# Row blocks coupled across tile and batch ends, and a new order of seats and gathered rows between dense and expert products

## The chip, the cores and the metric

The kernel runs on one core of one Trainium2 chip. The metric is the device time of one execution in microseconds (us). TensorE is PE in the rows (PEld: its weight loads), VectorE DVE, ScalarE ACT, GpSimd POOL, and SyncE, which issues most DMAs, SP.

## The reference

Four batches of attention with 12 heads, 448 rows, head size 64, whose scores are mixed over the heads before the softmax and whose weights are mixed after it; then a dense layer pair with ELU on 1792 tokens; then eight experts, each token to one or to none.

```python
scores = scale * np.matmul(q, k.transpose(0, 1, 3, 2))
scores = np.einsum('bhij,hg->bgij', scores, w_pre)
attn = np.exp(scores - np.max(scores, axis=-1, keepdims=True))
attn = attn / (np.sum(attn, axis=-1, keepdims=True) + 1e-09)
x = np.matmul(np.einsum('bhij,hg->bgij', attn, w_post), v)   # rows of 768
h = x @ w_in
x = np.where(h > 0.0, h, np.exp(np.minimum(h, 0.0)) - 1.0) @ w_out
# where x @ w_skip > 0: e = argmax(x @ w_gate), p = its softmax weight
out = x + p * (np.maximum(x @ w1[e], 0.0) @ w2[e])           # else x
```

## The kernel before

**Attention.** A tile is 120 query rows of a batch, or its last 88 (`ROWS`): 16 tiles `T`. `qk` (L153) makes the scores of two heads ("a pair", six a tile) and moves them, one head on ScalarE, one on VectorE, into `st[T]`; two such buffers alternate. Mixing over heads is done on row blocks of up to 10 rows (`blocks_of`, L76): `relayout` (L187) brings a block with its 12 heads onto the partitions by DMA, `mix_pre` (L201) multiplies two blocks, a *couple* `U`, with the spread-out mixing matrix, `top`, `softmax` and `norm` do the rest, and `mix_post` (L251) mixes again, transposed, into two PSUM tiles `f`, whose blocks `move` copies to `att[T]`. `av` (L275) multiplies two heads' weights with the values. The 88-row tile was cut into eight blocks of 10 and two of 4.

A *unit* `n` of the loop (L399) is up to two couples of one tile, three units a tile, so the last unit of each batch has one couple. TensorE's order in a unit, by hand: `mix_pre` of its couples, `mix_post` of the former unit's first couple, one `av`, two `qk`, `mix_post` of the former unit's second couple. `when` gives by division which tile's pairs, keys and queries are due. `split_k` and `high_q`/`low_q` split keys and queries in two parts. `qk` and `mix_pre` share four PSUM buffers `w` in turn. In the last five units (`late`) the score pools are closed (`scoring.close`) and the dense layer is begun in steps (`next(mix)`): weights are loaded (L530), narrowed (L541 to L553), x is loaded and split. Each engine works in order; up to `order.close()` (in the dense layer) the order is that of the program, behind it a scheduler's, which `behind` (an instruction goes out after a named one) holds.

**Between dense and expert products.** The second dense product goes by tiles of 128 tokens (L918). For each tile `route` picks the expert, `seat` (L829) counts how many earlier tokens go there (`ones` x `seen`), adds those of its tile (`upper` x one-hot), and scatters the token to its slot. Expert 0's first 128 rows are not read back from memory alone: `xp` holds rows gathered for the first 12 tiles, and the rows of tile 12 (`OLD`) and tile 13 (`LAST`) are added by products with a 0/1 place matrix `hot` (`place_old`, L884, and L963) in PSUM `pt`, 12 instructions each. The last tile's logits go over transposed copies (`score_turned`, `logits`).

## Time and profile before

| | us |
|---|---|
| timed runs | 994.80, 988.57, 992.12 |
| median | 992.12 |
| profiled execution | 988.09 |
| its span, first to last instruction | 986.2 |
| TensorE / VectorE / ScalarE / GpSimd busy | 963.5 / 722.0 / 550.9 / 233.5 |
| mean granted clock of TensorE | 0.996 of full speed |

The profile is one execution. A busy share is an average over stages with different limits, and the end of a matmul is modelled, so a busy TensorE is not one at its peak. In a timeline a row tells the start, the length, the engine, the line and operation, what it writes and reads, how many were merged, and in brackets how long its engine stood idle before it and who ended that. Units of the loop are told apart by the first `mix_pre` of each (L206).

### The profile page before, as it was taken

Reading aid. Unit: us, or ns where it says so; the run is one execution under the profiler, and the core shown is the slowest. Engines: PE = TensorE matmul, PEld = TensorE weight load, DVE = VectorE, ACT = ScalarE, POOL = GpSimd, SP = SyncE. Lnnn points to the kernel's source line nnn. Section 1 sums busy time; section 2 is a strip of 40 time slices with the busy share of each in tenths; the row PEclk is TensorE's granted clock in tenths of the full one; section 3 lists DMA queues with packets and bytes.
Section 4 is the critical chain, followed back from the end, with each engine's and each line's share of the span. In section 5 each row is a group of like instructions: output and inputs, shape, how many; then the busy total and the mean of one; then the engine's idle time right before and its main releaser. Section 6 shows DMA issues by size and latency. Waiting matters only on the chain. (4 is left out here: it accounts for less than half of the span.)

```text
span 986.2 us, 30114 instructions
## 1 busy us (share of the span) xinstructions
PE 963.5 (98%) x12286; PEld 838.7 (85%) x12286; DVE 722.0 (73%) x1458; ACT 550.9 (56%) x1113; POOL 233.5 (24%) x291
## 2 busy tenths in 40 slices
PE   9999999999998999999999999999999999999996
PEld 4677777777776789998999999999999998898985
DVE  6777777777776786666666478877686847999973
ACT  4887788788786754444554453222212106788861
POOL 2333234234222322223233100010100004252001
PEclk9999999999999999999999999999999999999999
DMA  6674674574557565445666389643333387999910
GB/s 202 219 237 145 216 234 156 198 240 153 195 190 234 175 207 184 157 161 169 219 225 211 137 292 290 175 126 97 118 97 100 104 294 264 394 394 397 391 71 34
DMA packets 129160, 199.86 MB, mean 203 GB/s; under 512 B 31924, under 2 KB 95863, under 8 KB 128764
## 3 DMA queue, kind: packets, MB, share of 16 engines
q1 hardware_dynamic: 126812, 191.60, 58.1%
q0 software_dynamic: 2160, 6.31, 1.7%
q8 instruction: 97, 1.59, 0.7%
q14 instruction: 43, 0.35, 0.1%
q10 hardware_dynamic: 48, 0.00, 0.0%
HBM read 122.66 MB, written 37.35 MB: 162 GB/s over the span
## 5 line engine op out<-in xcount | busy, mean ns | idle before, releaser
L918 PE MATMUL o<-w,gh 128*128 128x384 f32 (+2 forms) x1344 | 238.2, 336 | 0.0
L636 PE MATMUL h<-xh,w 128*128 128x448 f32 x1152 | 235.4, 366 | 1.6 <-DVE xh L572 1.3
L918 PEld LDWEIGHTS o<-w,gh 128*128 128x128 f32 x1344 | 232.0, 188 | 2.2
L636 PEld LDWEIGHTS h<-xh,w 128*128 128x128 f32 x1152 | 215.7, 188 | 20.2 <-DVE xh L572 1.9
L214 DVE TENSOR_REDUCE nmx<-c 128x1 f32<-128x448 f32 x184 | 102.3, 617 | 51.9 <-PE c L206 51.8
L266 PEld LDWEIGHTS f<-kr,e 64*64 64x64 f32 x5888 | 105.3, 135 | 36.6 <-issue 22.3
L227 ACT ACTIVATE e<-c,nmx 128x448 f32<-128x448 f32 x184 | 114.5, 633 | 25.5 <-DVE nmx L214 25.4
L805 DVE SCALAR_TENSOR_TENSOR junk<-x,wrow 128x768 f32<-128x768 f32 x117 | 111.8, 955 | 18.4 <-ACT x L948 12.8
L247 POOL TENSOR_SCALAR kr<-kpost,rs 128x60 f32<-128x60 f32 x184 | 79.4, 455 | 183.9 <-DVE rs L242 90.6
L1086 DVE TENSOR_TENSOR wlo<-w1t,whi 128x1536 fp32r<-128x1536 f32 x64 | 110.8, 1751 | 10.7 <-ACT whi L1084 8.9
L266 PE MATMUL f<-kr,e 64*64 64x60 f32 (+1 forms) x5888 | 108.3, 219 | 2.9 <-issue 1.8
L553 POOL TENSOR_TENSOR wf<-a,p 128x768 f32<-128x768 f32 x32 | 66.1, 2066 | 181.1 <-DVE p L551 139.4
L1084 ACT CAST whi<-w1t 128x1536 fp32r<-128x1536 f32 x64 | 93.8, 1483 | 21.5 <-PE y L1126 9.4
L790 ACT CAST gh<-gr 128x512 fp32r<-128x512 f32 x56 | 34.8, 624 | 97.1 <-PE o L918 35.5
L206 PE MATMUL c<-d,kpre_low 64*64 64x448 f32 x368 | 84.1, 547 | 0.3 <-DMA d<-s 0.2
L206 PE MATMUL c<-d,kpre_up 60*64 60x448 f32 x368 | 81.6, 548 | 0.0
L272 ACT COPY at<-f 128x420 f32<-128x420 f32 (+1 forms) x136 | 65.6, 518 | 28.0 <-PE f L266 27.2
L294 PE MATMUL xp<-at,v 128*64 128x120 f32 (+1 forms) x1152 | 67.1, 264 | 3.1 <-issue 3.0
L853 POOL DMA_INDIRECT slots<-pairs,si x14 | 18.9, 1348 | 204.6 <-DVE si L852 152.7
L166 PE MATMUL qk<-k,qq 64*120 64x448 f32 x504 | 65.3, 381 | 0.7 <-ACT e L227 0.2
L294 PEld LDWEIGHTS xp<-at,v 128*64 128x64 f32 x1152 | 56.1, 137 | 10.6 <-issue 9.3
L170 ACT ACTIVATE s<-qk 120x448 f32<-120x448 f32 x96 | 52.2, 548 | 23.1 <-PE qk L166 14.6
(204 smaller groups left out, 1278.7 us busy)
## 6 DMA issues: line engine op xcount, KB each, us to landing
w1t<-in_moe_w_dram SPq DMA_DIRECT2D x64, 768.0 KB
d<-s SPq DMA_DIRECT2D x176, 210.0 KB
gT<-g SPq DMA_DIRECT2D x64, 224.0 KB
f<-in_moe_w_in_dram SPq DMA_DIRECT2D x16, 768.0 KB
f<-in_moe_w_out_dram SPq DMA_DIRECT2D x16, 768.0 KB
gr<-gT SPq DMA_DIRECT2D x48, 256.0 KB
rq<-in_q_dram SPq DMA_DIRECT2D x15, 360.0 KB
rk<-in_k_dram SPq DMA_DIRECT2D x24, 224.0 KB
```

Source lines behind the costliest of these rows:

```text
L206: nc.tensor.matmul(out=ps[j * UP:(j + 1) * UP, :S], lhsT=kpre_up[UP:UP + HP, :] if z else kpre_low, rhs=d[z, j])
L214: nc.vector.tensor_reduce(out=t, in_=c, op=ALU.max, axis=AX.X, negate=True)
L227: nc.scalar.activation(out=e, in_=c, func=ACTF.Exp, bias=t, accum_out=sms[0][:, k + i:k + i + 1])
L247: nc.gpsimd.tensor_scalar(out=kr, in0=kposts[z], scalar1=rs[:, 2 * i + z:2 * i + z + 1], scalar2=None, op0=ALU.mult)
L266: nc.tensor.matmul(out=ps[to, heads, z, :], lhsT=e[rows, keys * JW:(keys + 1) * JW], rhs=kr[rows, first * HR:(first + n) * HR])
L294: nc.tensor.matmul(out=ps[i][z * 64:(z + 1) * 64, :n], lhsT=vt[b, p][:, jc * 2 + z, :], rhs=att[T][:, jc * H + ORDER.index(2 * p + z), :n] ...
L553: nc.gpsimd.tensor_tensor(out=w, in0=a, in1=p, op=ALU.add)
L636: nc.tensor.matmul(out=ps, lhsT=w[:, a, kk, :], rhs=xs[tb, kk][:, z, :], start=(kk == 0 and a + z == 0), stop=(kk == NK - 1 and a == 1))
L805: nc.vector.scalar_tensor_tensor(out=t[:, o:o + n], in0=x2, scalar=1.0, in1=w, op0=ALU.mult, op1=ALU.mult, accum_out=lg[:, e:e + 1])
L918: mm = nc.tensor.matmul(out=po[c][:, :cols[c].stop - cols[c].start], lhsT=gs[i][fc // GC][:, a, fc % GC, :], rhs=wo[fc][:, z, cols[c]], st ...
L1084: nc.scalar.copy(out=hi, in_=t)
L1086: nc.vector.tensor_tensor(out=lo, in0=t, in1=hi, op=ALU.subtract)
```

## The change

Blocks of a tile are 10 rows and one rest (12, 12, 12, 9 a batch). Couples and units are cut from the whole list of blocks, whatever tile or batch a block is of: 180 blocks, 90 couples, 45 units of two couples. `begins` and `ends` tell the first and last couple of a tile; from them two lists are made: `pairs_in` (which score pairs a unit computes: two, in six units three, none in the last five) and `values_in` (which `av`: one, twice two, three in the last unit). Loads and splits of keys and queries follow `pairs_in`. A `mix_post` writes its two blocks where each belongs. In unit 40 both relayouts of unit 42 are issued before the score pools close, so unit 41 issues none of them. The `av` in the last unit after the first two uses two of the buffers `w`.

Behind the dense products `place_old` is cut in two: `place_pre` (the gathered rows `xp`, no place matrix needed) and `place_old` (tile 12's rows). `seat` is cut too: `counted` makes the product with `seen`, and in `seat` the place matrix comes ahead of the sums' rest; the weight's reciprocal (`weigh`) is put behind it for tiles 12 and 13. All products of the stage are put in one order by `behind`: two of `place_pre`, transposes, the seat product of tile 12, two of `place_pre`, logits, the last two of `place_pre`, two of `place_old`, the seat products of tile 13, four of `place_old`, then the products of tile 13's rows.

```diff
-    whole = n // BR * BR
-    few = (n - whole) // 2
-    return [(r, BR) for r in range(0, whole, BR)] + [(whole + i * few, few) for i in range(2 if few else 0)]
+    return [(r, min(BR, n - r)) for r in range(0, n, BR)]
...
         blks = [(T, r, m) for T in range(len(tiles)) for r, m in blocks_of(ROWS[tiles[T][1]][1])]
-        units = []
-        for T in range(len(tiles)):
-            Gs = [G for G in range(len(blks)) if blks[G][0] == T]
-            Us = list(zip(Gs[::2], Gs[1::2]))
-            units += [Us[2 * u:2 * u + 2] for u in range(3)]
+        Us = list(zip(range(0, len(blks), 2), range(1, len(blks), 2)))
+        units = [Us[i:i + 2] for i in range(0, len(Us), 2)]
         NP = len(units)
+        begins = [[T for T, _, _ in blks].index(T) // 2 for T in range(len(tiles))]
+        ends = [U - 1 for U in begins[1:]] + [len(Us) - 1]
+        for T in range(1, len(tiles)):
+            if blks[2 * begins[T]][0] != T:
+                ends[T - 1] = begins[T]
...
+
+        pairs_in, values_in = {}, {}
+        for T in range(1, len(tiles)):
+            n1 = begins[T] // 2 - (2 if begins[T] % 2 else 3)
+            n0 = n1 - 2
+            if T > 1:
+                gone = ends[T - 2]
+                n0 = max(n0, gone // 2 - (1 if gone % 2 else 2), max(pairs_in) + 1)
+            if T == len(tiles) - 1:
+                n1 -= 1
+            ns = range(n0, n1 + 1)
+            for p in range(NK):
+                pairs_in.setdefault(ns[p * len(ns) // NK], []).append((T, p))
+        for T in range(len(tiles) - 1):
+            n0 = max(ends[T] // 2 + 2, max(values_in, default=0) + 1)
+            n1 = min(begins[T + 2] // 2 + 1 if T + 2 < len(tiles) else NP - 1, n0 + 2)
+            for u in range(3):
+                values_in.setdefault(min(n0 + u, n1), []).append((T, u))
...
                 T, r, m = blks[G]
-                whole = ROWS[tiles[T][1]][1] // BR * BR
-                t = r // BR if r < whole else (whole // BR) + (r - whole) // m
-                rows = st[T][:PR].rearrange("(a t) h s -> t a h s", a=BR)[t][:m]
+                rows = st[T][:PR].rearrange("(a t) h s -> t a h s", a=BR)[r // BR][:m]
...
-            T, r, m = blks[U[0]]
-            if r == 0:
-                att[T] = at_p.tile([128, NA, 120], FP32, tag="at", name="at")
+            for G in U:
+                if blks[G][1] == 0:
+                    att[blks[G][0]] = at_p.tile([128, NA, 120], FP32, tag="at", name="at")
...
             def move(copy, j):
+                T, r, m = blks[U[j]]
...
                 first = HR - m // 2
-                copy(out=to[:, :, r + j * m:r + (j + 1) * m], in_=at[:, :, first:first + m])
+                copy(out=to[:, :, r:r + m], in_=at[:, :, first:first + m])
...
-        def when(n):
-
-            return n // 3, n % 3
-
+        def first_in(n):
+
+            return [T for T, p in pairs_in.get(n, ()) if p == 0]
+
+        def fresh(n):
+
+            return [(tiles[T][0], p) for T, p in pairs_in.get(n, ()) if tiles[T][1] == 0]
...
             new = units[n + 1] if n + 1 < NP else ()
-            T, u = when(n + 5)
-            T1, u1 = when(n + 6)
-            T2, u2 = when(n + 7)
-            for U in new[1:]:
-                relayout(U)
+            now = pairs_in.get(n, [])
+            new_q = [(T, p // 2) for T, p in now if T >= PLAIN and (T, p // 2) not in qt]
+            new_q = [x for i, x in enumerate(new_q) if x not in new_q[:i]]
+            if n != NP - 4:
+                for U in new[1:]:
+                    relayout(U)
             store()
-            if n == NP - 5:
-                scoring.close()
...
             del values[:2 if n else 0]
-            if T2 < len(tiles):
-                if u2 == 0:
-                    load_q(T2)
-                if tiles[T2][1] == 0:
-                    load_k(tiles[T2][0], 2 * u2)
-                    load_k(tiles[T2][0], 2 * u2 + 1)
-            if PLAIN <= T < len(tiles):
-                high_q(T, u)
+            for T in first_in(n + 2):
+                if T > 1:
+                    load_q(T)
+            for b, p in fresh(n + 2):
+                load_k(b, p)
+            for x in new_q:
+                high_q(*x)
...
                     relayout(units[n + 2][0])
+            if n == NP - 5:
+                relayout(units[n + 2][1])
+                scoring.close()
...
                 top(U)
-            if PLAIN <= T < len(tiles):
-                low_q(T, u)
+            for x in new_q:
+                low_q(*x)
...
             moves, scores = [mix_post(U) for U in old[:1]], []
-            weighted = [av((n - 1) // 3 - 1, (n - 1) % 3)] if n >= 4 else []
-            if T < len(tiles):
-                scores.append(qk(T, 2 * u))
+            weighted = [av(*x) for x in values_in.get(n, ())[:1]]
+            if now:
+                scores.append(qk(*now[0]))
...
                 next(mix)
-            keys = (tiles[T1][0], 2 * u1, nc.gpsimd) if T1 < len(tiles) and tiles[T1][1] == 0 else ()
+            keys = [(*bp, nc.gpsimd) for bp in fresh(n + 1)]
             if n < 3:
-                keys = 0, 2 * n, nc.vector
-            if keys:
-                split_k(*keys)
+                keys = [(0, 2 * n + i, nc.vector) for i in range(2)]
+            for x in keys[:1]:
+                split_k(*x)
...
                 f()
-            if T < len(tiles):
-                scores.append(qk(T, 2 * u + 1))
+            for f in scores[:len(now) - 2]:
+                f()
+            scores = scores[max(len(now) - 2, 0):]
+            for x in now[1:]:
+                scores.append(qk(*x))
...
                 f()
-            if keys:
-                split_k(keys[0], keys[1] + 1, keys[2])
+            for x in keys[1:]:
+                split_k(*x)
...
                 m[0](nc.scalar.copy)
-            if n == NP - 1:
-                av(n // 3 - 1, n % 3)()
+            for i, x in enumerate(values_in.get(n, ())[1:]):
+                av(*x, *([[ps_w.tile([128, 512], FP32, tag="w", name="xp") for _ in range(2)]] if i else []))()
...
                 nc.scalar.activation(out=ex, in_=lg[:, :E], func=ACTF.Exp, bias=nmx, accum_out=sm)
-                nc.vector.tensor_scalar(out=sm, in0=sm, scalar1=1e-9, scalar2=None, op0=ALU.add)
-                nc.vector.reciprocal(out=pairs[:, i, 1:2].bitcast(FP32), in_=sm)
-                return i, oh, do
-
-            def seat(i, oh, do, after=None):
+
+                def weigh(after=None):
+                    with behind(after):
+                        nc.vector.tensor_scalar(out=sm, in0=sm, scalar1=1e-9, scalar2=None, op0=ALU.add)
+                    nc.vector.reciprocal(out=pairs[:, i, 1:2].bitcast(FP32), in_=sm)
+                if i < OLD:
+                    weigh()
+                return i, oh, do, weigh
+
+            def counted(i, oh, do, weigh, after=None):
...
                     nc.tensor.matmul(out=pp[:, :E], lhsT=ones, rhs=seen, start=True, stop=False)
+                return i, oh, do, weigh, after, pp
+
+            def seat(i, oh, do, weigh, after=None, pp=None):
+
+                if pp is None:
+                    pp = counted(i, oh, do, weigh, after)[-1]
                 with behind(after):
-                    nc.tensor.matmul(out=pp[:, :E], lhsT=upper, rhs=oh, start=False, stop=True)
-                nc.vector.tensor_tensor(out=seen, in0=seen, in1=oh, op=ALU.add)
+                    seated[i] = nc.tensor.matmul(out=pp[:, :E], lhsT=upper, rhs=oh, start=False, stop=True)
...
                                                accum_out=sl)
+                place = None
+                if i >= OLD:
+                    place = wg_p.tile([128, 128], FP32, tag=f"hot{i}", name="hot")
+                    made = nc.vector.tensor_scalar(out=place, in0=iota128, scalar1=sl, scalar2=do, op0=ALU.is_equal,
+                                                    op1=ALU.mult)
+                    weigh(made)
+                nc.vector.tensor_tensor(out=seen, in0=seen, in1=oh, op=ALU.add)
...
                                         op1=ALU.add)
-                place = None
-                if i >= OLD:
-                    place = wg_p.tile([128, 128], FP32, tag=f"hot{i}", name="hot")
-                    nc.vector.tensor_scalar(out=place, in0=iota128, scalar1=sl, scalar2=do, op0=ALU.is_equal,
-                                            op1=ALU.mult)
...
+            seated, started, hots = {}, [], []
...
-            def place_old(ks):
+            def place_pre(ks, after):
...
                 for k in ks:
-                    col = slice(k * 128, (k + 1) * 128)
-                    o = pt[k // 3][:, k % 3, :]
-                    nc.tensor.matmul(out=o, lhsT=xp[:, col], rhs=ident, start=(k % 3 == 0), stop=False)
-                    nc.tensor.matmul(out=o, lhsT=rows[LAST - 1][:, col], rhs=old_hot, start=False, stop=False)
-
-            def logits(turned):
+                    with behind(after):
+                        done = nc.tensor.matmul(out=pt[k // 3][:, k % 3, :], lhsT=xp[:, k * 128:(k + 1) * 128], rhs=ident,
+                                                start=(k % 3 == 0), stop=False)
+                return done
+
+            def seat_old():
+
+                hots.append(seat(*started[0]))
+                return seated[OLD]
+
+            def place_old(ks, after):
+
+                for k in ks:
+                    with behind(after):
+                        done = nc.tensor.matmul(out=pt[k // 3][:, k % 3, :],
+                                                lhsT=rows[LAST - 1][:, k * 128:(k + 1) * 128], rhs=hots[0],
+                                                start=False, stop=False)
+                return done
+
+            def logits(turned, after=None):
                 for k, t in turned:
-                    nc.tensor.matmul(out=lg[:, :E + 1], lhsT=t, rhs=wgt[:, k, :], start=(k == 0), stop=(k == NK - 1))
-
-            def score_turned(x2, c):
+                    with behind(after):
+                        done = nc.tensor.matmul(out=lg[:, :E + 1], lhsT=t, rhs=wgt[:, k, :], start=(k == 0),
+                                                stop=(k == NK - 1))
+                return done
+
+            def score_turned(x2, c, mm):
...
                     with behind(mm):
-                        nc.tensor.transpose(p[:, j], x2[:, k * 128:(k + 1) * 128], ident)
+                        done = nc.tensor.transpose(p[:, j], x2[:, k * 128:(k + 1) * 128], ident)
                 copied = nc.scalar.copy(out=t[:, :len(ks)], in_=p[:, :len(ks)])
-                return [(k, t[:, j]) for j, k in enumerate(ks)], copied
+                return [(k, t[:, j]) for j, k in enumerate(ks)], copied, done
...
                 if last and n == len(halves) - 5:
-                    turned, _ = score_turned(x2, 0)
+                    turned, _, _ = score_turned(x2, 0, mm)
...
                 if i and n == (AT_ROUTE if last else AT_OLD if i == OLD else AT_SEAT):
-                    hot = old_hot = seat(*routing, None if last else mm)
+                    if last:
+                        started.append(counted(*routing, mm))
+                    else:
+                        seat(*routing, mm)
...
                         if last and c == 1:
-                            turned, freed = score_turned(x2, c)
-                            place_old(range(2))
-                            logits(turned)
-                            place_old(range(2, 4))
+                            placed = place_pre(range(2), mm)
+                            turned, freed, done = score_turned(x2, c, placed)
+                            with behind(done):
+                                done = seat_old()
+                            done = place_pre(range(2, 4), done)
+                            done = logits(turned, done)
+                            done = place_pre(range(4, NK), done)
+                            done = place_old(range(2), done)
...
                             nc.sync.dma_start(out=out[i * 128:(i + 1) * 128, :], in_=x2)
-            hot = seat(*route(NTILE - 1, lg))
-            place_old(range(4, NK))
+            hot = seat(*route(NTILE - 1, lg), done)
+            place_old(range(2, NK), seated[LAST])
...
```

## Rows read from the trace of the kernel before

**Rows 1.** Page, part 1: busy us (share of span) and instructions of TensorE

```profile
PE 963.5 (98%) x12286; PEld 838.7 (85%) x12286; DVE 722.0 (73%) x1458; ACT 550.9 (56%) x1113; POOL 233.5 (24%) x291
```

**Rows 2.** Windows by stage: length, busy us (instructions) per engine, clock, DMA share, GB/s

```profile
42.31:297.61 255.30, 252.06 (x7132) 192.14 (x7125) 186.51 (x423) 206.51 (x546) 82.12 (x170) 1.00 0.59 195
...
815.86:822.75 6.89, 6.07 (x50) 5.38 (x48) 3.17 (x32) 3.23 (x8) 1.02 (x1) 1.00 0.63 241
...
822.75:976.90 154.15, 153.18 (x949) 136.68 (x948) 137.08 (x155) 112.99 (x113) 43.16 (x23) 1.00 0.78 292
```

**Rows 3.** Windows: two full units, one with a single couple

```profile
147.86:154.38 6.52, 6.52 (x204) 4.98 (x198) 4.87 (x11) 6.10 (x17) 3.30 (x6) 1.00 0.59 198
...
160.91:167.44 6.53, 6.53 (x204) 4.99 (x198) 4.88 (x11) 5.29 (x14) 1.66 (x5) 1.00 0.43 154
...
167.44:173.71 6.27, 6.24 (x197) 4.70 (x190) 3.95 (x9) 4.05 (x10) 1.00 (x3) 1.00 0.75 222
```

**Rows 4.** Timeline, TensorE, a full unit: start, length, engine, line, operation, out<-in, count

```profile
154.38 0.57 PE L206 MATMUL c<-d,kpre_low 64*64 64x448 f32 x1
...
155.91 1.08 PE L266 MATMUL f<-kr,e 64*64 64x60 f32 x64
...
156.82 0.42 PE L288 MATMUL xp<-at,v 64*64 64x120 f32 x8
...
158.55 1.48 PE L166 MATMUL qk<-k,qq 64*120 64x448 f32 x12
...
159.96 1.13 PE L266 MATMUL f<-kr,e 64*64 64x60 f32 x64
```

**Rows 5.** Timeline, TensorE, the last units; in brackets the idle time before

```profile
325.75 1.32 PE L266 MATMUL f<-kr,e 64*64 64x60 f32 x64 [0.98 <-POOL kr L247]
...
336.81 0.38 PE L288 MATMUL xp<-at,v 64*64 64x88 f32 x8 [0.53 <-ACT at L272]
```

**Rows 6.** Groups by line, ScalarE: count, busy us, mean ns, idle before

```profile
L170 ACT ACTIVATE s<-qk 120x448 f32<-120x448 f32 x96 | 52.2, 548 | 23.1 <-PE qk L166 14.6 <-PE qk L162 6.2
...
L143 ACT CAST qq<-rq 128x240 fp32r<-128x240 f32 x42 | 16.9, 402 | 0.0
...
L137 ACT CAST k<-rk 128x448 fp32r<-128x448 f32 x24 | 13.9, 577 | 0.0
```

**Rows 7.** Timeline, SyncE's queue: relayouts of a unit, two weight loads

```profile
141.84 3.42 SPq L198 DMA_DIRECT2D d<-s  x4
...
300.57 0.36 SPq L530 DMA_DIRECT2D f<-in_moe_w_in_dram  x1
...
339.26 0.43 SPq L530 DMA_DIRECT2D f<-in_moe_w_in_dram  x1
```

**Rows 8.** Timeline, ScalarE: first use of those two loads

```profile
307.80 0.91 ACT L541 ACTIVATE a<-f 128x768 f32<-128x768 f32 x1
...
346.03 0.91 ACT L541 ACTIVATE a<-f 128x768 f32<-128x768 f32 x1 [0.94 <-DMA f<-in_moe_w_in_dram]
```

**Rows 9.** Timeline, TensorE, end stage: last seat product, last placing products

```profile
820.23 0.29 PE L835 MATMUL pp<-oh,upper 128*128 128x8 f32 x2
...
821.35 1.50 PE L963 MATMUL pt<-hot,x 128*128 128x128 f32 x12
```

**Rows 10.** Timeline, VectorE, end stage: last tile's maximum and one-hot

```profile
817.88 0.17 DVE L811 MAX8 mx<-lg 128x8 f32<-128x8 f32 x1 [1.53 <-PE lg L894]
...
818.97 0.29 DVE L819 TENSOR_SCALAR oh<-iota,ef,do 128x8 f32<-128x8 f32 x1
```

**Rows 11.** Timeline, TensorE, unit 44

```profile
310.14 0.67 PE L294 MATMUL xp<-at,v 128*64 128x120 f32 x3 [2.80 <-issue]
...
310.74 1.93 PE L266 MATMUL f<-kr,e 64*64 64x60 f32 x64
```

**Rows 12.** Windows: the stretch after that wait (granted clock after the engines)

```profile
309.90:313.30 3.40, 3.16 (x75) 2.35 (x78) 1.33 (x2) 0.56 (x2) 1.53 (x4) 0.50 0.97 267
```

**Rows 13.** DMA queues, 300 to 314 us: packets, MB, share of 16 engines

```profile
q8 instruction: 3, 0.05, 1.5%
```

## Prediction of the time after the change

> **What bounds the kernel now.** I read the page first: TensorE (PE) is busy 963.5 of 986.2 us [rows 1]. That is a modelled busy time, so I went on to stretches, to see whether PE really sets the pace. In the middle of the attention, units 4 to 42, PE is busy 252.06 of 255.30 us and ScalarE (ACT) 206.51; between the dense and the expert products it is 6.07 of 6.89; in the experts 153.18 of 154.15 [rows 2]. Then single units: a full one takes 6.53 us whether ACT has 5.29 us of work in it or 6.10 [rows 3], so PE sets it and ACT has some 0.4 to 1.2 us to spare. Last the PE timeline of one full unit [rows 4]: the two `mix_pre` take 154.38 to 155.91, 0.77 us a couple; one `mix_post` 155.91 to 156.82 and the other 159.96 to the next unit at 160.91, 0.93 on average; the weighted sum 1.73; two score pairs 1.41, 0.70 each. They fill the unit; there is no hole to win, only work to drop. The profiled execution took 988.09 us, span 986.2; the three timed runs have a median of 992.12, 4.03 more. I work out a difference against the profiled one and put it on the median.
>
> **The change part by part.**
>
> *Fewer couples.* Blocks of a tile were 12, in the last tile of a batch 10 (two of 4 rows): 46 a batch, 184, 92 couples, 48 units, four of them with one couple. Now blocks are 12, 12, 12 and 9, a couple may hold blocks of two tiles, a unit couples of two tiles or batches: 180 blocks, 90 couples, 45 units, all full. Weighted sums, score pairs and stores stay as many; they fall into three units fewer. Two couples go: 2 x (0.77 + 0.93) = 3.4 us less PE work.
>
> *Short units go.* A unit with one couple should take 6.53 - 0.77 = 5.76 us; it took 6.27 [rows 3], because its short `mix_pre` gives the normalised kernels from GpSimd too little time. Such units stand three times in the middle: 3 x 0.51 = 1.5 us less. The fourth is the last unit: there PE waited 0.98 us for those kernels [rows 5]; a second `mix_pre` covers 0.77 of it: 0.7 less. Bounds for both together: 0 (the wait moves to another unit) to 2.5.
>
> *Three score pairs in a unit.* By the planner's lists six units (7, 8, 30, 31, 38, 39) hold three pairs instead of two. The four PSUM buffers then come round: the third pair takes the first pair's, so PE, in order, waits until ACT and VectorE have moved the first out, and the second `mix_post` is queued behind. One such eviction is 0.55 us on ACT [rows 6]; the second pair's 0.70 us of PE work hides it if ACT starts at once. Bounds 0 to 0.55 each; I take 0.15, since ACT is done with its exponentials by then: 0.9 more (0 to 3.3).
>
> *Casts of keys.* With a new batch in units 7 and 30 a unit has three casts (0.58 each) instead of two, one eviction and one cast of queries (0.40) more: 6.10 + 0.58 + 0.55 + 0.40 = 7.63 us on ACT against 6.52 + 0.70 = 7.22 on PE [rows 3, 4, 6]. ACT becomes the bound there by 0.4: 2 x 0.4 = 0.8 more (0, if units 8 and 31, without casts, take it up, to 3.0, if all of the added 1.53 is paid twice).
>
> *Handover of score buffers* I cost at nothing: the relayouts that read a tile's old scores for the last time are issued, at the latest, in the first half of the unit in which the next scores of that buffer are written, and those come last but one in a unit [rows 4]. Where that cover is gone, ACT and VectorE wait about one issue, 3.42 / 4 = 0.86 us [rows 7], four times at most, and PE only for what their spare time leaves.
>
> *The late units.* Before unit 40 ends both relayouts of unit 42 must be issued, and the region of the scores closes behind them. So on SP the first load of dense weights stands behind two more issues of 3.42 / 4 = 0.86 us each, 1.7 us later. In the kernel before it was issued at 300.57 and used at 307.80, 7.23 us later; a like load issued at 339.26 was only just there at 346.03, 6.77 us, and ACT waited 0.94 for it [rows 7, 8]. So 0.46 us are spare, and I charge 1.7 - 0.46 = 1.2. Behind ACT's instruction VectorE's sums, GpSimd's kernels and PE's next `mix_post` are queued. Bounds 0 (their own slack takes it) to 1.7.
>
> *The end of the attention.* The last unit now leaves two couples for the tail instead of one. The PSUM pair of `mix_post` has two buffers, so the second couple waits for the first one's evictions, as the weighted sum did, 0.53 us [rows 5], with one hand-over more than that: 0.6. The last weighted sum now uses the buffers that the first dense product takes over, about one copy, 0.4. Together 1.0 more (0 to 1.5).
>
> *Seats and gathered rows.* In the end stage PE runs in order, and the last tile's seat product started at 820.23 though its one-hot, begun at 818.97 and 0.29 long, was there at 819.26: 0.97 us behind eight instructions that place the old tile's rows [rows 9, 10]. That one-hot itself comes 1.09 us after the maximum at 817.88, fourteen steps on VectorE, eight of them the old tile's: at most 8/14 of it, 0.62, of which I take two thirds, 0.42, since an instruction's own inputs leave gaps. The change takes the old tile's seat ahead of the logits, fills PE's waits with the gathered rows, and leaves eight of the old tile's twelve instructions for the time in which VectorE turns seats into the last place matrix (820.23 to 821.35, 1.12 us; they take 0.88). I take 0.97 + 0.42 = 1.4 less. Bounds 0 to 0.97 + 0.62 = 1.6 (0.82 of it PE shows as idle [rows 2]). The experts follow PE all through, so the gain lasts to the end.
>
> Sum: -3.4 - 1.5 - 0.7 + 0.9 + 0.8 + 1.2 + 1.0 - 1.4 = -3.1 us. 988.09 would be 985.0; 992.12 becomes 989.0.
>
> **A long stall in the late units.** In unit 44 PE stood 2.80 us "issue", waiting for nothing that the profile shows; the instructions after it took 1.93 instead of 1.13 us [rows 11], with the granted clock at 0.50, the 1.2 GHz level, for 3.40 us [rows 12]. That is 2.8 + 1.7 = 4.5 us. In the same 14 us three packets of the instruction queue moved while the DMA engines were full [rows 13]; I read the stall as instructions that came late, and leave it in both kernels, since the same loads stand in the same steps. The Trainium skill (Runtime: NRT & Kernel Launch, section Instruction fetch mechanics) says that the sequencer fetches blocks of 16 KiB through its own queue and that this is mostly hidden; by that the stall belongs to one unlucky place and would go with the new order, and the time would be 984.5. No trace here separates the two.
>
> **The rivals.**
> 1. *The stall goes.* The late units are laid out anew, and nothing ties the stall to a step of the program. For it: other units show only waits well under 1 us. Against it: the same weights and inputs are loaded there, past the same full engines. 989.0 - 4.5 = 984.5; with the best bounds of the sum, down to 980.
> 2. *ACT eats the gain.* If the wait for PSUM is 0.55 in all six units and the added casts are paid in full: 2.4 + 2.2 more, 993.6. For it: ACT has 0.4 us to spare in a unit with casts. Against it: neighbours without casts have 1.2.
> 3. *The dense weights come late* (slower than before). Place: ACT's narrowing instruction in the late units, ahead of VectorE's sums in their queues. Two weight loads fall there. It decides once a load lands more than some 3 us after that instruction is due: then PE stands as long as in [rows 11] and loses the clock as in [rows 12], 4.5 us a load. Both: 989.0 - 1.2 + 9.0 = 996.8. For it: the spare 0.46 us. Against it: the two extra issues explain 1.7, not 3.
> 4. *The end stage doesn't move*: the scheduler already fills PE, 990.4. It lies within my own range and shares its chance.
>
> **How the numbers follow.** My forecast with its own range 985 to 991.5: 0.55. Rival 1: 0.18. Rival 2: 0.15. Rival 3: 0.12, of which a third goes past 1002, where clock and fetch stalls add up. The range 982 to 996 leaves the ends of rivals 1 and 3 out, about 2 in 10. About 1% is what a measurement of this kernel can tell from no change: faster by over 1% means under 982.2, the better half of rival 1 with a fraction of the forecast, 0.12; slower means over 1002.0, 0.05; within, 0.83.
>
> **What would show it.** Right: 90 couples of `mix_pre` instead of 92 and no short unit; full units still 6.5 us; units 7, 8, 30, 31, 38, 39 at 7.2 to 7.7; units 4 to 39 near 249 us (255.30 for 4 to 42 [rows 2], less three couples, 5.1, a weighted sum, 1.7, and the short units, 1.5, plus the 1.7 of pairs and casts); the stage from the last dense product to the first expert product near 5.5 instead of 6.89 us. Wrong: PE waits for evictions or kernels over 1 us in the six units; ACT's narrowing waits for its load; a stretch at clock 0.50 that comes, goes or doubles.

## The result, and the profile after

The changed kernel takes 1004.55 us (median of 4 runs, 1002.07 to 1006.43), the kernel before 991.83 (4 runs, 988.57 to 994.80): a ratio of 1.0111, 95% interval 1.0072 to 1.0151. I had forecast 989.0 with a range of 982 to 996. The change makes the kernel slower: the two medians stand 12.7 us apart, by the ratio it is 11. Most of that comes from the part that I had booked as a gain.

The profiled execution of the changed kernel took 1006.43 us, its span is 1004.7. First the stages, as the windows by stage show them (length, busy us with instructions of each engine, granted clock, DMA share, GB/s): units 4 to 39, the last five units up to the first dense product, the stage between dense and expert products, and the first 154.15 us of the experts. They answer to [rows 2].

```profile
43.96:295.57 251.61, 244.45 (x6885) 185.27 (x6878) 181.62 (x407) 200.98 (x531) 79.43 (x164) 1.00 0.59 195
...
295.57:337.84 42.27, 35.49 (x960) 27.08 (x951) 24.72 (x54) 25.77 (x66) 12.59 (x21) 0.88 0.63 183
...
826.55:832.20 5.65, 5.63 (x49) 5.32 (x47) 3.39 (x32) 3.13 (x8) 1.02 (x1) 1.00 0.78 294
...
832.20:986.35 154.15, 146.91 (x849) 131.47 (x849) 134.62 (x152) 111.99 (x111) 41.38 (x22) 0.97 0.78 289
```

The kernel before, last five units in the same view:

```profile
297.61:331.30 33.69, 29.38 (x920) 22.36 (x910) 22.77 (x48) 24.00 (x62) 11.60 (x20) 0.95 0.70 208
```

Read them one by one. The middle fell from 255.30 to 251.61 us. The stage between dense and expert products fell from 6.89 to 5.65, and PE no longer idles in it (5.63 busy of 5.65). But in the same 154.15 us of the experts PE has issued 849 products instead of 949 and was busy 146.91 us instead of 153.18: the stage that I had only moved forward lost time itself, 9.0 us up to the end of the span (172.5 instead of 163.5). And the last five units take 42.27 us instead of 33.69; 2.5 us of that is work that the new order moved there out of the middle, the `mix_pre` of one more couple (0.77) and one more weighted sum (1.73).

The timeline of PE shows where it stood (start, length, line, out<-in; in brackets the idle time and what ended it), and the windows below it the stretches at clock 0.50, the 1.2 GHz level.

```profile
199.28 0.56 PE L283 MATMUL f<-kr,e 64*64 64x60 f32 x24 [2.89 <-issue]
...
309.85 0.67 PE L283 MATMUL f<-kr,e 64*64 64x60 f32 x32 [2.27 <-POOL kr L264]
310.84 1.08 PE L283 MATMUL f<-kr,e 64*64 64x60 f32 x32 [0.32 <-POOL kr L264]
...
325.12 1.33 PE L283 MATMUL f<-kr,e 64*64 64x60 f32 x40 [3.04 <-issue]
...
850.71 1.65 PE L1188 MATMUL y<-whi,ht 128*128 128x384 f32 x4 [6.99 <-DVE ht L1165]
```

```profile
310.50:313.90 3.40, 3.08 (x60) 2.76 (x58) 3.08 (x6) 2.79 (x9) 1.09 (x3) 0.50 0.79 242
...
324.10:330.90 6.80, 5.78 (x120) 4.53 (x123) 3.17 (x6) 2.72 (x7) 1.96 (x4) 0.50 0.55 169
...
846.30:856.50 10.20, 5.79 (x18) 5.80 (x19) 8.35 (x24) 1.78 (x2) 6.78 (x5) 0.50 0.85 296
```

The kernel before had one such wait and one such stretch before the dense products [rows 11, 12]; after, there are two, and a third in the experts that is new. That third one is the largest: PE waits 6.99 us for the turned hidden rows of expert 0, and from within that wait on the clock is halved for 10.2 us. Follow the chain back through GpSimd, VectorE and SyncE (same view, one line for each engine's step):

```profile
829.13 1.02 POOL L890 DMA_INDIRECT slots<-pairs,si  x1 [2.64 <-DVE nmx L846]
833.47 2.46 POOL L890 DMA_INDIRECT slots<-pairs,si  x1 [3.31 <-DVE xt L1028]
839.77 0.61 POOL L1299 DMA_DIRECT2D ids<-slots  x1 [3.84 <-DMA slots<-pairs,si]
...
833.33 3.42 DVE L1148 TENSOR_TENSOR wlo<-w1t,whi 128x1536 fp32r<-128x1536 f32 x2
...
848.15 0.17 DVE L1112 TENSOR_TENSOR swapped<-ids 128x8 int32<-128x8 int32 x1 [7.51 <-DMA ids<-slots]
...
835.14 7.88 SPq L1135 DMA_DIRECT2D w1t<-in_moe_w_dram  x6
```

PE's hidden rows are turned by VectorE; VectorE stands 7.51 us at the first step of `reorder()`, which reads the ids; the ids are loaded by GpSimd only after the last scatter into `slots` has landed; that scatter took 2.46 us to issue and a further 3.84 until the loads could go. In between, at 835.14, SyncE began a burst of weight loads. In the kernel before, the same scatter started at 822.81, 0.06 us after the first expert product, took 0.97 us, and the ids were requested at 825.21, half a microsecond before the burst at 825.69. The chain had won a race that nobody had written down; after the change it loses it.

### The profile page after: what moved, and what is told of

The parts are those of the page before. It is cut to its first block, busy times and chain, and to the rows that moved or that the text cites. A ratio compares the mean times of both kernels' runs of the same rounds, so it can differ in the third digit from the quotient of the medians.

```text
span 1004.7 us, 29771 instructions
## 1 busy us (share of the span) xinstructions
PE 969.4 (96%) x12142; PEld 842.0 (84%) x12142; DVE 720.0 (72%) x1447; ACT 547.4 (54%) x1103; POOL 232.3 (23%) x287
## 5 line engine op out<-in xcount | busy, mean ns | idle before, releaser
L661 PE MATMUL h<-xh,w 128*128 128x448 f32 x1152 | 238.0, 368 | 1.6 <-DVE xh L597 1.1
L231 DVE TENSOR_REDUCE nmx<-c 128x1 f32<-128x448 f32 x180 | 100.1, 617 | 52.6 <-PE c L223 52.6
L244 ACT ACTIVATE e<-c,nmx 128x448 f32<-128x448 f32 x180 | 111.8, 634 | 23.4 <-DVE nmx L231 23.3
L169 DVE TENSOR_SCALAR s<-qk 120x448 f32<-120x448 f32 x96 | 58.3, 622 | 9.8 <-PE qk L164 5.5
```

The source lines that it names most:

```text
L231: nc.vector.tensor_reduce(out=t, in_=c, op=ALU.max, axis=AX.X, negate=True)
L244: nc.scalar.activation(out=e, in_=c, func=ACTF.Exp, bias=t, accum_out=sms[0][:, k + i:k + i + 1])
L661: nc.tensor.matmul(out=ps, lhsT=w[:, a, kk, :], rhs=xs[tb, kk][:, z, :], start=(kk == 0 and a + z == 0), stop=(kk == NK - 1 and a == 1))
```

## The experiments

Single executions scatter: of the 31 runs of the kernel before beside the first four experiments 30 lie between 986 and 999 us and one at 1009. So times are given as medians and as ratios to the kernel before that ran beside them, and stages from profiles are compared over several kernels. The stages in the table are the starts of the units, of the first dense product, of the last output product's end and of the first expert product on PE's timeline.

| kernel | ratio to before (95%) | last five units | stage between | experts |
|---|---|---|---|---|
| before | | 33.7 | 6.9 | 163.5 |
| changed | 1.0111 (1.0072 to 1.0151) | 42.3 | 5.7 | 172.5 |
| changed, again | 1.0106 (1.0061 to 1.0152) | 39.6 | 5.7 | 171.8 |
| blocks only | 1.0012 (0.9975 to 1.0048) | 40.0 | 6.9 | 164.7 |
| end only | 1.0054 (1.0017 to 1.0091) | 34.5 | 5.7 | 164.4 |
| changed, early ids | 1.0004 (0.9972 to 1.0036) | 39.5 | 5.7 | 164.8 |
| end only, early ids | 1.0002 (0.9972 to 1.0033) | 34.1 | 5.7 | 162.5 |
| changed, cast behind scatter | 1.0006 (0.9977 to 1.0035) | 40.4 | 5.7 | 165.4 |
| before, early ids | 0.9989 (0.9964 to 1.0015) | 34.3 | 8.5 | 162.4 |

**One part alone.** Blocks only: the functions `blocks_of` and `attention` of the changed kernel with `mixtures` of the kernel before. End only: the other way round.

> The attention of the change (row blocks through tile and batch ends, the new planner of score pairs and weighted sums) with the dense and expert stages of the kernel before. Theory A (two separate losses: the late attention units with their late weight load, about +8 us between the start of the last five units and the first dense product, and the seats' transfer chain in the experts, +11 to +12): here only the first is left, the middle units keep their 3.7 us, so +4 to +6 us over the kernel before, and VectorE's first step of the swapped ids waits about as in the kernel before (1.2 us). Rival B (the new phase of the whole program, not the order of seats, throws the seats' transfers behind the weight loads): +11 to +13 us, and that VectorE wait is 6 us or more here too.

> The attention of the kernel before with the new order of gathered rows and seats. Theory A: the stage between dense and expert products is 1.4 us shorter, and PE then stands some 7 us for the hidden rows of expert 0 with the clock at its half level behind it: +8 to +11 us over the kernel before. Rival B (the loss in the experts comes with the phase that the new attention gives): -1 to -2 us.

Blocks only: 994.59 us against 993.55, ratio 1.0012 (0.9975 to 1.0048); VectorE waits 2.32 us for the ids. End only: 998.54 us, ratio 1.0054 (1.0017 to 1.0091). So the attention part costs about nothing, and the part that shortens a stage by 1.2 us makes the kernel slower by itself. Neither theory was quite right: in its profiled execution the end-only kernel did not lose the race, it won it narrowly, and PE's wait was 1.61 us, not 7:

```profile
831.12 0.97 POOL L865 DMA_INDIRECT slots<-pairs,si  x1 [3.01 <-DVE xt L1003]
833.52 0.61 POOL L1274 DMA_DIRECT2D ids<-slots  x1 [1.43 <-DMA slots<-pairs,si]
...
831.28 3.42 DVE L1123 TENSOR_TENSOR wlo<-w1t,whi 128x1536 fp32r<-128x1536 f32 x2
...
833.09 7.26 SPq L1110 DMA_DIRECT2D w1t<-in_moe_w_dram  x6
```

Compare this with the changed kernel, each against its first expert product (830.15 and 832.20 us). The scatter starts 0.97 us after it here and 1.27 there. Here it is 0.16 us ahead of VectorE's cast `wlo` and takes 0.97 us; there it is 0.14 us behind that cast and takes 2.46. Between these two profiles a start 0.3 us later goes with 5.4 us more of PE's wait. The other nine executions of this kernel lie between 993 and 1007 us, which would fit a race that goes either way, but they have no trace.

**The changed kernel again**, as a control beside the runs with the early ids:

> The changed kernel itself once more, beside the others on one chip, since single executions of one kernel scattered by up to 10 us in the first experiments. Theory (the chain of the seats' transfers is a race that the change mostly loses): executions scatter between about 995 and 1008 us, the median 6 to 11 us over the kernel before, and the profiled one shows either a last scatter that takes 2.2 us or more and lands 6 us after its start, with the experts at 171 to 173 us, or one that takes 1.0 us and lands after 2.1 us, with the experts at 164 to 165. Rival (the loss is a fixed cost of the new work): every execution within 2 us of 1004.

1001.70 us (998.40 to 1007.15, 6 runs), ratio 1.0106 (1.0061 to 1.0152). The profiled execution, 998.40 us, is the fastest of the six, and it too has lost the race: experts 171.8 us, the scatter 2.04 us after the first expert product, 1.69 us long. So the changed kernel loses in both of its profiles, neither shows the short landing that I had named as the other outcome, and the race is not what spreads its executions over 9 us.

**Take VectorE's wait away.** `reorder()` and the gather of expert 3 move behind the second products of expert 0:

```
             expert_first(0, h, jobs(((3, 2), turn_h, h, ht, 0)))
-            reorder()
-            xg[3] = gather(ids[3])
             expert_second(0, ht, jobs(((0,), turn_h, h, ht, 1), ((2,), turn_x, 1)))
+            reorder()
+            xg[3] = gather(ids[3])
```

> The changed kernel with the reordering of the ids (six VectorE steps that wait for the last load of ids) and the gather of expert 3 traced behind the second products of expert 0 instead of ahead of them. Theory (VectorE stood 7.5 us for the ids with the turned hidden rows queued behind it): the 7.0 us stall of PE and the half clock after it go, 10 to 12 us less than the changed kernel, so about the kernel before or 1 to 2 us over it. Rival (the transfers themselves are late, and PE meets the late gathered rows next): 0 to 5 us less, with PE waiting for the turned rows of expert 1.

998.39 us, ratio 1.0056 (1.0019 to 1.0092): about half of the loss stays. The profiled execution is the slowest of the ten (1004.42 us), with experts of 171.5 us, and it shows what the rival said. VectorE's wait is gone, PE's wait for the hidden rows is down to 1.48 us, and the stall stands at the next user of the same late transfers, the gathered rows:

```profile
853.80 1.51 PE L1163 MATMUL pt<-ident,xg 128*128 128x128 f32 x6 [4.36 <-DMA xg<-x2d,ids]
```

So in this execution `reorder()` is where the lateness shows, not where it comes from; why the median still fell by half of the loss has no trace.

**Take the burst out of the chain's way.** SyncE loads the ids itself, behind the thirteenth weight load and ahead of the fourteenth; then no load of the burst can start before the last scatter has landed:

```
             ahead(W_EARLY)
-            nc.gpsimd.dma_start(out=idt[:, 1:2], in_=by_expert[:, 1:2])
+            with behind(loaded[-1]):
+                nc.sync.dma_start(out=idt[:, 1:2], in_=by_expert[:, 1:2])
...
-            nc.gpsimd.dma_start(out=idt[:, 3:E], in_=by_expert[:, 3:])
+            held[0] = nc.sync.dma_start(out=idt[:, 3:E], in_=by_expert[:, 3:])
...
-                    with behind(wrow_in if len(raws) < R0 else None):
+                    with behind(wrow_in if len(raws) < R0 else held[0]):
```

> The changed kernel with the four loads of ids issued by SyncE behind the thirteenth load of expert weights and ahead of the fourteenth, instead of by GpSimd: no weight load can start until the last scatter of seats has landed. Theory (the scatter and the ids' loads stand behind the burst of weight loads): the scatter lands about 2 us after its issue ends, the ids within 2.5 us of their issue, VectorE's wait for the ids goes under 2.5 us, the experts fall from 172 to 163 to 166 us, and the time is 5 to 9 us under the changed kernel of the same runs. Rival 1 (the order of issues on GpSimd is late by itself): the landings stay at 5 us or more and the gain is under 2 us. Rival 2 (the weights become late instead): PE waits for casts of weights in expert 0 or 1, and the gain is under 3 us.

> The attention of the kernel before, the new order of seats and gathered rows, and the ids loaded ahead of the fourteenth weight load as in the run before. Theory (the end stage's 1.2 us are a real gain that the race takes back): 1 to 3 us under the kernel before, and 5 to 7 us under the version without the earlier ids (998.5). Rival (the new order costs more than the race): over the kernel before by 2 us or more.

> The kernel before with the ids loaded ahead of the fourteenth weight load, and nothing else. Theory (before, the last scatter lands ahead of the burst nearly always): within 2 us of the kernel before, experts at 163 to 165 us. Rival (the kernel before loses the race too in its slower executions): 2 to 4 us under it, with no execution above 1000 us.

The changed kernel falls from 1.0106 to 1.0004 (0.9972 to 1.0036), from 1001.70 to 994.32 us side by side, and its experts to 164.8 us. The timeline, and the window of the experts' first 154.15 us:

```profile
833.97 2.13 POOL L890 DMA_INDIRECT slots<-pairs,si  x1 [3.64 <-DVE xt L1028]
...
837.28 0.33 SPq L1301 DMA_DIRECT2D ids<-slots  x1
...
839.09 6.76 SPq L1135 DMA_DIRECT2D w1t<-in_moe_w_dram  x7
...
840.82 0.17 DVE L1112 TENSOR_TENSOR swapped<-ids 128x8 int32<-128x8 int32 x1
...
875.72 0.15 DVE L1205 TENSOR_SCALAR few_at<-few 128x1 int32<-128x1 int32 x1 [4.11 <-DMA few<-slots]
...
877.61 0.97 PE L1188 MATMUL y<-wlo,ht 128*128 128x384 f32 x4 [2.29 <-DVE wlo L1148]
```

```profile
832.38:986.53 154.15, 151.61 (x912) 135.52 (x915) 136.75 (x155) 112.93 (x113) 54.40 (x18) 1.00 0.79 297
```

The scatter is as late and as long as in the changed kernel (1.59 us after the first expert product, 2.13 us), but it lands 1.1 us after its issue ends instead of 3.6, and VectorE does not wait at all. The burst itself starts 3.8 us later than it did, and that has a price 45 us into the experts, a wait for a cast of weights as rival 2 had it, by another road. `few`, another small load from `slots`, stands behind the delayed loads in SyncE's queue and is issued 33 us after the first expert product, in the kernel before 26; VectorE waits 4.11 us for it, and PE 2.29 us for the cast of weights behind. The two other profiles with the new attention and the early ids have PE's wait there too (2.28 and 2.20 us), no other profile has it. With the old attention the same edit brings end only from 1.0054 to 1.0002 (0.9972 to 1.0033): not the 1 to 3 us under the kernel before that I had expected, but the interval reaches down to them. In the kernel before the same edit changes nothing that can be measured, 0.9989 (0.9964 to 1.0015); that execution happened to have a stage of 8.5 us between dense and expert products, with a granted clock of 0.80 over it, so that PE was busy 7.69 us in it and not 6.07.

**Take VectorE's cast out of the scatter's way.** All loads stay; VectorE may not begin the second to fourth cast of weights before GpSimd has issued the last scatter:

```
+            with behind(scattered[LAST]):
+                nc.gpsimd.memset(mark[:, 0:1], 0.0)
+            with behind(routed):
+                routed = nc.vector.tensor_copy(out=mark[:, 1:2], in_=mark[:, 0:1])
...
-                with behind(routed if early else None):
+                with behind(routed if 1 < n_parts[0] <= 4 else None):
```

> The changed kernel, all loads where they were, with VectorE held behind the issue of the last scatter: GpSimd clears a small tile right behind that scatter, VectorE copies it, and the next casts of expert weights follow that copy. Theory (GpSimd's issue of the scatter stands while a 1.75 us cast runs on VectorE; only that pushes it behind the burst of weight loads): the scatter takes 1.0 us instead of 1.5 to 2.6, lands 2 us after its start where it starts within 1.6 us of the first expert product, the experts take 164 to 167 us instead of 172, and the time is 4 to 8 us under the changed kernel (994 to 998), with some executions still slow where the scatter before it lands late. Rival (the burst of loads decides alone): the scatter takes 1.0 us and still lands 5 us or more after its start, experts 171 to 173 us, 1001 to 1005 us.

```profile
828.85 0.97 POOL L890 DMA_INDIRECT slots<-pairs,si  x1 [3.76 <-DVE xt L1029]
829.81 0.12 POOL L1031 MEMSET mark<- 128x1 f32 x1
831.25 0.61 POOL L1304 DMA_DIRECT2D ids<-slots  x1 [1.32 <-DMA slots<-pairs,si]
...
829.97 0.15 DVE L1033 COPY mark<-mark 128x1 f32<-128x1 f32 x1 [1.62 <-POOL mark L1031]
830.04 3.42 DVE L1153 TENSOR_TENSOR wlo<-w1t,whi 128x1536 fp32r<-128x1536 f32 x2
...
831.85 7.42 SPq L1140 DMA_DIRECT2D w1t<-in_moe_w_dram  x6
```

993.85 us, ratio 1.0006 (0.9977 to 1.0035), experts 165.4 us. The scatter starts even later than in the changed kernel (1.71 us after the first expert product) and is issued in 0.97 us, because VectorE is made to stand 1.62 us. The rest of the order of every engine is that of the changed kernel. A wait added, 10 us gained. But the hold delays the burst as well: the burst's first load goes out 0.06 us after the first of these casts of 1.75 us ends, here (831.79 and 831.85) as in the changed kernel (835.08 and 835.14), and so 4.7 us after the first expert product instead of 2.9. For the cast as the decisive part speaks that the scatter landed 3.8 us after the first expert product, and in the eight profiles whose burst is not held the first packets of the burst start 4.0 us after it; the loads of ids would have met them, as in blocks only and end only, where no cast catches the scatter and PE waits 1.8 and 1.6 us. So the burst is shown to be a necessary link of the loss, by the early ids; that the cast alone is the other is likely, and not shown, since no run takes it away and leaves the burst where it was.

**The late attention units.** Three experiments asked what the last five units lose.

> The changed kernel with ScalarE's and VectorE's first steps on the first dense weight moved behind the same unit's sums and evictions, all loads where they are. Theory (the sums of that unit were queued behind a load that came 1.9 us late): PE's waits of 2.27 and 0.32 us for the normalised kernels and the half clock after them go, 3 to 4.5 us less than the changed kernel. Rival (PE would have stood there in any case, for late instructions): under 1 us less, the stall shows as a wait for nothing visible one unit later.

The first steps of narrowing (ScalarE's `a`, VectorE's shift) move two hand-over points later, behind the unit's sums and evictions. 997.37 us, ratio 1.0045 (1.0009 to 1.0082): less than the changed kernel's 1.0106, but the intervals overlap, and the profiled execution was the longest of the ten (1011.5 us), so that only its waits are read:

```profile
316.11 0.56 PE L283 MATMUL f<-kr,e 64*64 64x60 f32 x24 [1.25 <-issue]
...
322.10 0.53 PE L223 MATMUL c<-d,kpre_low 64*64 64x448 f32 x1 [1.90 <-issue]
...
330.76 0.80 PE L283 MATMUL f<-kr,e 64*64 64x60 f32 x40 [3.32 <-issue]
```

No wait for normalised kernels is left, and two waits for nothing visible stand in its place. The one of 3.32 us is where the changed kernel has its 3.04: after the first 20 of the 64 records of unit 43's second `mix_post`.

> The changed kernel without the second load of dense weights and without the six loads of the second batch's inputs in the late attention units: it takes the first weights and the first batch's rows in their place, so that part of the dense products is of the wrong numbers; all other work is done, and 2.1 MB less moves in the last four units. Theory (PE's instructions come late there because the transfers of the late units fill the DMA engines): the wait of 2.5 to 3.3 us for nothing visible in the second last unit's second products goes or falls under 1 us, the stage from the start of the last five units to the first dense product falls from 39 to 42 us to 33 to 36. Rival (the lateness hangs on the instructions themselves, or on the traffic that stays): the wait stays at 2 us or more at the same products, and the stage stays within 2 us.

```profile
319.14 1.14 PE L283 MATMUL f<-kr,e 64*64 64x60 f32 x62
...
322.28 1.32 PE L283 MATMUL f<-kr,e 64*64 64x60 f32 x64 [0.41 <-POOL kr L264]
```

With 2.1 MB less to move, that wait is gone, and the last five units take 36.3 us instead of 39.5 to 42.3. A wait of 1.27 us at the start of unit 43, ahead of which nothing was left out, stays. The time, 1003.11 us, shows none of it: this kernel loses the race in the experts too (171.9 us), and what the late units give back is under the scatter of four runs.

> The changed kernel with the early ids, and 31 tiny products more on PE at the very start (34 of one column in place of three of the six that warm it up), so that every later instruction of PE stands some 62 records further back in its stream. Theory (PE waits where a block of its instructions ends, and a block is about 125 of the trace's product records): the wait of 2.5 to 2.9 us after the 20th of 60 products of the second last unit's second couple moves to a place about 62 records earlier in the program, the second last unit's score kernels or the weighted sum before them, and the packets of the instruction queue keep their distance of about 125 records; the time may move by 3 us either way. Rival (the wait belongs to that couple, for example its evictions): it stays at the same products.

```profile
309.25 0.33 PE L283 MATMUL f<-kr,e 64*64 64x30 f32 x4 [3.04 <-issue]
...
316.11 1.02 PE L283 MATMUL f<-kr,e 64*64 64x60 f32 x57 [0.55 <-issue]
...
320.33 0.36 PE L283 MATMUL f<-kr,e 64*64 64x60 f32 x10 [0.86 <-issue]
```

A unit of this stretch has 176 product records: 16 of `mix_pre`, 64 of a `mix_post`, 32 of the weighted sum, 64 again. In the changed kernel the wait stands 16 + 64 + 32 + 20 = 132 records into unit 43; here one stands 16 + 54 = 70 records into it, 62 earlier, and the one at unit 43's start has become one 57 records ahead of unit 42's end. Both are short now, 0.86 and 0.55 us; a long one of 3.04 us is at the border before them, in the last four records of unit 41, where three profiles of the unshifted stream have a wait 54 records into unit 42 (1.13 to 1.53 us). So the waits belong to places in PE's instruction stream and not to a couple's work, and how long one is depends on the traffic that the place meets. 995.33 us, ratio 1.0037 (1.0004 to 1.0069): no gain from this shift.

**Spread loads**, on top of the early ids: narrowing late as above, and the inputs of the dense products loaded mostly one at a time.

> The changed kernel with the ids loaded ahead of the fourteenth weight load, and in the late attention units ScalarE's first step on the dense weights moved behind that unit's sums, and the twelve loads of inputs issued mostly one at a time over the units instead of in twos and fours. Theory (the late units lose to transfers that come in bursts, beside PE's instructions and the first weights): the stage from the last five units to the first dense product falls from 39.5 to 34 to 37 us, the wait for normalised kernels goes under 0.3 us, and the time is 2 to 5 us under the version with the early ids alone, 988 to 992 us. Rival (the late instructions follow the bytes, not the bursts): the stage stays at 38 to 41 us with waits of 2 us or more for nothing visible, the time within 1 us of that version.

992.62 us, ratio 0.9997 (0.9971 to 1.0023); the last five units 37.2 us instead of 39.5 in the version with the early ids alone (windows of those units, this kernel first, then the early ids alone):

```profile
295.90:333.08 37.18, 31.04 (x960) 24.32 (x951) 24.35 (x54) 25.78 (x66) 12.18 (x21) 1.00 0.67 208
```

```profile
298.31:337.83 39.52, 33.19 (x961) 25.70 (x951) 24.50 (x54) 25.66 (x66) 12.80 (x21) 0.91 0.66 196
```

The clock stays whole, PE's wait in unit 43 is 1.65 us instead of 2.92, the wait for kernels is gone, but three other waits of 1.1 to 1.5 us for nothing visible remain: the late instructions follow the bytes more than the bursts. The stage is just outside what the theory had named, 34 to 37 us, and by the ratios the time is 0.7 us under that of the early ids alone, which is the rival's. This version is level with the kernel before. No version that I ran beats both kernels by more than the measurement can tell.

## Why the prediction was wrong, step by step

*Fewer couples, short units, three pairs, casts of keys.* As forecast in kind and nearly in size. GpSimd's 180 normalised kernels, two a couple, count the 90 couples; no short unit is left; twelve full units take 6.52 or 6.53 us, units 23 and 34, which hold two weighted sums each, 8.25 and 8.26; of the six units with three pairs five take 7.53 to 7.63 and unit 30 takes 8.59 with a wait for nothing visible of 0.73. Units 4 to 39 took 251.61 us, forecast 249; the wait of 2.89 us in unit 26 alone is more than that difference. Over the other profiles of this attention but the one of 1011.5 us the stretch takes 249.4 to 255.8 us, and over the four of the old attention, with three units more, 255.3 to 262.8. So the sum's -3.4 and -1.5 are in the traces by their sign, and not to the microsecond.

*The late weight load, +1.2.* The mechanism was right, its size depends on the execution. The load stands behind four relayouts, and not only behind their issue: SyncE, ScalarE and VectorE of the changed kernel:

```profile
296.58 3.47 SPq L215 DMA_DIRECT2D d<-s  x4
301.59 0.35 SPq L555 DMA_DIRECT2D f<-in_moe_w_in_dram  x1
...
307.41 0.89 ACT L566 ACTIVATE a<-f 128x768 f32<-128x768 f32 x1 [1.92 <-DMA f<-in_moe_w_in_dram]
...
308.33 0.56 DVE L569 TENSOR_SCALAR a<-a 128x768 int32<-128x768 int32 x1 [3.83 <-ACT a L566]
```

Between the last relayout's issue (300.05) and the load SyncE stands 1.54 us: its buffer lies in the region that the scores give up, and it goes out 0.14 us after the third relayout has landed (301.45 by the trace's semaphore records). This stand is 1.5 to 1.7 us in all ten profiles of the new attention and 0.2 in the four of the old. I had counted issues, 1.7 us, and not the landing. The load is issued 6.0 us into unit 40 where the kernel before issued it 3.0 us into its unit, and PE waits 2.27 and 0.32 us ([rows 7, 8] for the kernel before). In four other profiles of the same attention PE's two waits sum to 1.1 to 1.2 us, in one to 2.9. So 1.2 was a fair middle, and rival 3's place was right; its price of 4.5 us a load was nearly met twice, in the execution shown (2.6 us of waits and about 1.5 for the halved clock) and with the early ids (2.9 us, and the clock halved for 3.4 us behind them).

*The long stall, "left in both kernels".* This step failed by one stall. It does stay, and it is a fixed place of the program: with the old attention PE waits ahead of the last 3 of the 24 records of one weighted sum in four of four profiles (2.80, 3.35, 2.21, 2.55 us), with the new one after the 20th record of unit 43's second `mix_post` in all eight profiles that have neither the shifted stream nor the missing loads (1.65 to 3.32 us). But with the new order PE stands at borders of instruction blocks ahead of that one too: 1.1 to 3.2 us more in units 42 and 43, except in the two profiles where PE waited over 2.5 us for the kernels at that time anyway. The shifted stream and the missing loads, one profile each, show both conditions, the place and the traffic. The rule that I had cited from the Trainium skill ("Runtime: NRT & Kernel Launch", section "Instruction fetch mechanics"), that crossing a block is mostly hidden, holds for the middle units, where some 55 blocks a profile pass with none to three waits of 1 us or more for nothing visible; it does not hold here, and the stall did not go, as I had made of it in rival 1, with a new order.

*The end of the attention, +1.0.* From the start of the first dense product to that of the second it takes 10.36 us instead of 8.26; 0.93 of that is a `mix_post` that moved there, so 1.2 us were added.

Taken together the late units and the tail ate what the middle had gained, and the attention part is level with before (1.0012), where its terms had summed to -1.7. This difference is within that measurement.

*Seats and gathered rows, -1.4.* The stage shrank by 1.24 us, close to the term. The step that failed is the sentence after it: "The experts follow PE all through, so the gain lasts to the end." The experts also follow a chain that does not run through PE: the old tile's scatter, its landing, the last scatter, its landing, the ids, `reorder()`. I had worked out what the edit does to PE and VectorE and had left GpSimd's queue out of the sum, although the edit brings the first expert product 1.24 us nearer to the last output product, and the old tile's scatter only 0.8 (2.58 instead of 3.40 us behind it). What the runs showed in its place is a race with three runners, and each can be read off:

1. The last scatter starts 0.77 us after the scatter before it has landed, in all fourteen profiles (both write `slots`; the landings are those of the trace's semaphore records, and the brackets that name VectorE's `xt` name an instruction that has no such fixed distance). That landing waits for the weight loads that were issued before the end stage: it comes 0.6 us after the last large packet of these loads, in all fourteen, and they drain at a time of their own. Against the first expert product the old tile's scatter lands at -0.7 us in the kernel before, at +0.1 with the new attention and the old end, at +0.2 and -0.2 with the new end and the old attention, and at +0.5 to +2.1 in the nine profiles that have both. The 1.24 us by which PE comes earlier are in this difference. Why the new attention adds another 0.5 us or more stays open.
2. VectorE's first cast of weights that runs with the experts starts 1.1 us after the first expert product. A scatter that has begun by then, or that no cast meets, takes 0.97 or 0.98 us (six profiles). One that begins while such a cast runs ends 0.84 to 0.86 us after that cast, in eight of eight profiles, and so takes 1.5 to 2.6 us. The Trainium skill ("SBUF — State Buffer", section "Who interferes with whom") says that a VectorE instruction with two SBUF inputs contends with a GpSimd instruction that reads SBUF, through a port pair that the two share and that is an exclusive lock. The traces agree for a scatter that comes second, which stands until the cast has ended (and then ends while the next cast already runs). They do not show the reverse: in blocks only and end only the scatter began 0.3 and 0.2 us ahead of the cast, and the cast began 1.1 us after the first expert product and took 1.75 us, as elsewhere. The run that makes VectorE wait shows the scatter short again without the cast.
3. SyncE's burst starts 2.9 us after the first expert product, 0.06 us after that cast has ended. So a scatter that the cast has caught, and that ends 0.85 us after the cast, always comes behind the burst's start. A scatter that has been issued by then lands 1.1 us after its issue ends; one issued later, with the burst running, lands 3.3 to 4.2 us after, and the loads of ids take 5.2 to 6.7 us in the changed kernel instead of 1.7 to 2.2 where the burst waits for them. In the kernel before only the first of them was ahead of the burst, 2.0 us, and the others took 3.9 to 5.5.

Lost, it costs PE 6.99 us, and from within the wait on the clock is at 1.2 GHz for 10.2 us, with PE busy 5.79 us in them: about 3 more. That is the order of the 9.0 us by which the experts grew, and of the 10 us that either cure gives back. Chance, not only size, was wrong here: all four rivals dealt with PE, ScalarE, VectorE and the dense weights, and none with the transfers between the two stages, so "slower by over 1%" had 0.05.

Last, the base. The profiled execution of the kernel before was 4 us under its median; later executions of it reach from 986 to 1002 us, and one 1009. A forecast of 3 us was always going to be small against that.

## What to carry to other kernels

When an edit makes a stage shorter, ask what else needed the time that it took: list every chain that starts in that stage, through every queue, with the moment at which the next user needs its end, and look for the place where it passes a burst of loads by less than the edit saves. A chain of small dependent transfers belongs ahead of the bulk loads by an order that is written down, not by timing; here four loads on another queue were worth 10 us, more than the whole rewrite of the attention. Then look at the next small load behind the bulk that was pushed back; here it cost 2.3 us. And where a stage can stall in two ways, compare several profiles before a stall is put down to an edit.

## What the hardware showed that I had not expected

- GpSimd's issue of an indirect DMA stands still during a 1.75 us cast on VectorE: 0.97 or 0.98 us alone or begun before the cast, 1.5 to 2.6 us when it begins in one, always ending 0.84 to 0.86 us after the cast (eight profiles).
- PE's instructions come in packets of 16 KB, 96 of them for the changed kernel's 12142 product records, so one for about 125. Over the fourteen profiles each of PE's 47 waits of 1 us or more for nothing visible, in the middle and in the late units, ended 1.3 to 1.7 us after the end of such a packet. In the late units, with DMA shares of mostly 0.7 to 1.1, PE so stood 1.7 to 3.4 us at one place, the same in every profile of the same attention whose stream is not shifted and whose loads are all there.
- In the changed kernel's profile a stretch of 3.4 to 10.2 us at a granted clock of 0.50 began within or right behind each wait of 2.6 to 7 us on PE in the late units and in the experts' first part; half of PE's busy time in those stretches, 1.5 to 2.9 us, comes on top of the wait. No such stretch belongs to the wait of 2.89 us in unit 26 (clock 1.00 over the middle).
